# A delta-rule attention and router kernel: triangular inversions joined in pairs, in the room of the first expert's weights

## The chip, the cores and the metric

The kernel runs on one core of one Trainium2 chip. A core has a matrix engine (TensorE, PE), three engines for elementwise work (VectorE or DVE, ScalarE or ACT, GpSimd or POOL) and a queue that mostly issues DMA transfers (SyncE, SP). The metric is the device time of one execution in microseconds. Several executions are made, and their median is the time of a kernel. The profile is of one execution, and it has its own time and its own span.

## The reference

Everything is float32. First an attention block with a state: 4 batches, 8 heads, 768 tokens, head dimension 48. Each head carries a 48 by 48 state that is changed at every token:

```python
k_n = k / (np.linalg.norm(k, axis=-1, keepdims=True) + 1e-06)
for t in range(S):
    kt, vt, bt = (k_n[:, :, t], v[:, :, t], beta[:, :, t, None])
    y[:, :, t] = np.einsum('bhd,bhde->bhe', q[:, :, t], state)
    v_old = np.einsum('bhde,bhd->bhe', state, kt)
    state = state + bt[:, :, :, None] * np.einsum('bhd,bhe->bhde', kt, vt - v_old)
```

The result, put together over the heads, is `x` with 3072 rows of 384. Then comes a mixture of 8 experts. A router computes `x @ w_gate + log1p(exp(x @ w_noise)) * noise` for each row and takes the two largest; their weights are a softmax over the two. An expert computes `relu(x @ w1[e]) @ w2[e]` with 1024 hidden values, and each row's output is the weighted sum of its two experts.

## The kernel before

**Chunks, units, steps.** The attention is computed in chunks of 64 tokens. Inside a chunk the recurrence becomes a triangular system; between chunks only the state is carried. A unit is one chunk of two batches with all heads (128 rows), so each of the 12 chunks has 2 units. Two chunks are a step: 6 steps of 4 units.

**Work of a unit.** PE transposes k (L594, copied by ACT at L601) and multiplies k with itself (L612). The products' 32 by 32 blocks on the diagonal go to `gd` (L645), those beside it to `at`. After the inversion, `join` (L821, L827) puts two 32-blocks together to a 64-block; `within` transposes q and forms the masked products `qk` (L864). `recur` is the part that depends on the state: the old state's part of v (L612, then a subtraction on DVE, L914), the state's part of the answer (L885), the solve (L930, copied by ACT at L941), the gather of the new state (L952) and its addition on DVE (L964). v is multiplied by the norms of k on POOL (L894). `answer` computes the rows (L989), stores them to `rows_y`, turns them (L999) and multiplies them with the router's weights (L1004).

**The inversion.** One step's triangular blocks are inverted on DVE for all 32 units and heads at once. `gd` is transposed in 32 by 32 blocks into `t` (L662). A few small operations find the length of each k (L683 to L704), POOL clears one triangle (L712), a scale follows (L731), and then 30 columns of two instructions each: a product into `part` (L743) and an addition to `t` (L747). After the ends (L756, L759), two transposes write `tb` (L770) and `tt` (L778), which `join` reads. The list `INVERSIONS` says which steps are inverted together, as pairs of first step and number of steps; the tile `t` has a dimension for that number. Before, it is six times one step:

```python
INVERSIONS = [(s, 1) for s in range(6)]
```

**Routing and early tiles.** `route(g)` runs after some of the steps (`ROUTES`: after step 1, 3, 4 and 5, counted from 0). It picks the experts of the rows so far and scatters row numbers and weights into `tokens_x` with indirect DMAs on POOL (`spread`, L437, two per unit). The first five row tiles of expert 0, the early tiles, are computed in the same list of work: their metas are loaded, their rows gathered (L401), turned (L1294), multiplied (L1313), put through relu (L1324), multiplied back (L1337) and weighted (L1349). `put_early` adds a tile to the output.

**The order of work.** All of this is a list of jobs in the class `Jobs`. Each job has an engine, a cost, what it reads and writes, and perhaps a due time. `order` is a planner: it goes through a modelled time, and on each engine takes the job with the smallest key among those that can start. `FIRST`, `PACE` and `BEHIND` give the due times, `SLOW` multiplies PE's costs, and `PATIENCE`, `SOON`, `AFTER` and `APART` adjust the choice. The order that comes out is written to all five queues as it stands, so an instruction that waits holds back whatever is behind it on its engine. Buffers for kp, kT, v, q, norms and others are rings of fixed lengths. The weights of expert 0, `w1e` and `w2e` (1.5 MB each), are loaded during step 3. The output is cleared by four transfers (`clear_out`), and `blanks` fills `tokens_x`.

**After attention.** `rest()` is the seam: it loads the metas of all experts, gathers the remaining rows of expert 0 (`rest_x`) and the rows of expert 1 (`load_rows`), regroups them in sixteen transfers (L1562), forms sums of weight blocks on POOL, makes the puts that were held back, and multiplies the rest of expert 0 (L1686, L1697, L1707, L1712). Experts 1 to 7 follow with a scheme that needs fewer products (L1548).

Of the kernel before, what the change touches and what calls it, by code (L numbers as in the profile page):

```python
# [9 lines left out]
FP32 = mybir.dt.float32  # L10
# [11 lines left out]
Q = 32  # L22
# [5 lines left out]
EARLY_TILES = 5  # L28
PUT_IN_RULE = 1
# [6 lines left out]
FIRST, PACE, BEHIND = 15.0, 44.0, 110.0  # L36
INVERSIONS = [(s, 1) for s in range(6)]
# [59 lines left out]
class Jobs:  # L97
# [9 lines left out]
    SLOW = 1.3  # L107
# [5 lines left out]
    def add(self, engine, cost, emit, reads=(), writes=(), opens=None, uses=None, closes=None,  # L113
            lands=0.0, moves=0.0, due=None, late=None, apart=0.0):
# [3 lines left out]
            due=1e9 if due is None else due, late=late, apart=apart, after=set(),  # L118
# [24 lines left out]
    def order(self):  # L143
# [4 lines left out]
        for job in jobs:  # L148
            job.key = (0, job.due) if job.late is None else (1, job.late)
# [5 lines left out]
        ready = [0.0] * len(jobs)  # L155
# [66 lines left out]
    AFTER = 5.0  # L222
    APART = 2.0
    PATIENCE = 0.02
    SOON = 8.0
# [8 lines left out]
def kernel(  # L234
# [178 lines left out]
    early_x = [const.tile([128, DM], FP32, name=f"early_x{i}") for i in range(4)]  # L413
# [52 lines left out]
    def deltanet(ictx):  # L466
# [34 lines left out]
        NK, NT_, NW = 3 * US, 3 * US - 1, US + NU  # L501
# [21 lines left out]
        gd_all = sb([128, UH, Q], "gd")  # L523
        most_steps = max(x for _, x in INVERSIONS)
        inversion_of = {s + x: g for g, (s, n) in enumerate(INVERSIONS) for x in range(n)}
        t_invs = ring([128, most_steps, Q, Q], "t", 2)
        parts = sb([128, most_steps * 240], "part")
        tts, tbs = sb([128, UH, Q], "tt"), sb([128, UH, Q], "tb")
        norms = ring([128, UH], "norms", 3)
# [10 lines left out]
        def load_beta():  # L540
            by_block = beta.rearrange("(u b) h (s c n j) -> b n c u h s j", b=2, c=2, n=2, j=Q)
            for i in range(128 // H):
                b, n, c, u = i // 8, i // 4 % 2, i // 2 % 2, i % 2
                jobs.add(
                    SP, 0.7,
                    lambda i=i, at=(b, n, c, u): nc.sync.dma_start(  # L546
# [5 lines left out]
        def load(n, name):  # L552
            c, u = divmod(n, NU)
            src, t, size = {"k": (k, kps, NK), "q": (q, qps, NQ), "v": (v, vs, NQ)}[name]
            if name == "k":
                for i in range(2):
                    for z in range(2):
# [3 lines left out]
                            engine, 0.5,  # L561
# [25 lines left out]
        def turned(n, name, src, size, to, to_size):  # L587

            p = bank(1, True)

            def emit():
                p_t = p.tile.rearrange("p (j t) -> p j t", t=128)
                for j in range(NP):
# [6 lines left out]
                ACT, 0.6,  # L600
                lambda: nc.scalar.copy(  # L601
                    to(n), p.tile.rearrange("p (j t) -> p j t", t=128)
                ),
# [17 lines left out]
        def products(n):  # L621
# [6 lines left out]
            p = bank(2, True)  # L628
# [9 lines left out]
            for x, lo in enumerate(range(0, 128, Q)):  # L638
                rows, cols = slice(lo, lo + Q), slice(lo % C, lo % C + Q)
                on, copy = (DVE, nc.vector.tensor_copy) if s == 0 and x % 2 else (  # L640
                    ACT, nc.scalar.copy
                )
# [609 lines left out]

        def flat(p):
            return p.tile if p.size == 1 else p.tile[:, 0]

        def early(s, lo, hi):


# [622 lines left out]
```

## Time and profile before

| what | value |
|---|---|
| times of the runs shown | 811.42, 812.33, 818.18 us; median 812.33 |
| the profiled execution's own time | 819.58 us |
| its span | 817.8 us |
| mean granted PE clock | 0.897 |
| PE busy | 727.6 us |
| DVE busy | 566.7 us |
| ACT busy | 311.6 us |
| POOL busy | 414.3 us |
| first early product (L1313) on the chain | 319.07 us |
| first product of expert 1 on the chain (L1548) | 395.57 us |

The span runs from the first to the last instruction in the trace; the execution's own time is 1.8 us longer. The profiled execution took 7.3 us more than the median. Lines such as L743 are lines of the kernel before. A busy PE is not a PE at its peak: the granted clock says how fast it ran, and 0.50 means that a matmul takes about twice as long as at 1.00. The names before and after the arrow in a row are the tile that is written and the tiles that are read.

### The profile page before, as it was taken

How to read it: one execution, taken by the hardware profiler on the slowest of the kernel's cores; microseconds unless marked ns; L12 is line 12 of the kernel's file. 1: busy time of each engine (PE TensorE's matmuls, PEld its weight loads, DVE VectorE, ACT ScalarE, POOL GpSimd, SP SyncE). 2: the span in 40 equal slices, each digit the busy share in tenths (PEclk: the TensorE clock that was granted, in tenths of full speed). 3: DMA queues.
4: the chain of work that ended last, by engine and by line, in shares of the span. 5: the costliest groups of instructions: out<-in, count | busy, mean ns of one | idle time of the engine just before them, and what ended most of it. 6: DMA issues, size and time to landing. Idle time of an engine off the chain costs nothing.

```text
span 817.8 us, 22648 instructions
## 1 busy us (share of the span) xinstructions
PE 727.6 (89%) x9365; PEld 572.8 (70%) x9365; DVE 566.7 (69%) x1256; ACT 311.6 (38%) x740; POOL 414.3 (51%) x398
## 2 busy tenths in 40 slices
PE   4665887887889889999999999999999999999993
PEld 3445776676778779778568678578587597596693
DVE  4899889998899631303588487587686785785841
ACT  3547394846764542112250430430521511502500
POOL 2102100105520633569677786886886886787032
PEclk9955789768868656999999999999999999999998
DMA  2465636633333102464645444553445346333031
GB/s 47 78 111 126 184 96 157 175 73 67 61 72 71 43 23 40 156 105 84 183 112 120 126 132 83 146 154 56 144 142 104 100 138 129 89 59 43 0 38 26
DMA packets 142928, 79.61 MB, mean 97 GB/s; under 512 B 118624, under 2 KB 139232, under 8 KB 141792
## 3 DMA queue, kind: packets, MB, share of 16 engines
q1 hardware_dynamic: 128096, 57.94, 27.1%
q0 software_dynamic: 12544, 19.75, 13.7%
q8 instruction: 75, 1.23, 0.7%
q10 hardware_dynamic: 2176, 0.39, 0.3%
q14 instruction: 37, 0.30, 0.2%
HBM read 49.85 MB, written 20.03 MB: 85 GB/s over the span
## 4 chain that ended last, share of the span: by engine, by line
PE 60%; DVE 21%; issue 10%; POOL 3%; SPq 2%; ACT 1%; DMA 0%; DVEq 0%; POOLq 0%; ACTq 0%
PE inner L1548 25%; PE outer L1548 14%; DVE part L743 6%; DVE t L747 5%; PE pair L1313 3%; PE pair L1337 3%; PE pair L612 2%; POOL out_dram L456 2%; PE inner L1659 2%; PE single L1004 1%; SPq L546 1%; DVE t L662 1%; DVE qk L864 1%; PE pair L989 1%; SPq L562 1%
## 5 line engine op out<-in xcount | busy, mean ns | idle before, releaser
L1615 ACT ACTIVATE hT<-inner 128x416 f32<-128x416 f32 x112 | 57.9, 517 | 260.8 <-PE inner L1548 259.4
L1609 DVE TENSOR_TENSOR hT<-hT,inner 128x416 f32<-128x416 f32 x182 | 105.6, 587 | 64.0 <-PE inner L1548 55.9
L456 POOL DMA_INDIRECT out_dram<-sums,metas_x x51 | 83.6, 1639 | 94.4 <-DVE sums L1448 67.1
L437 POOL DMA_INDIRECT tokens_x<-meta,slot x48 | 48.7, 1014 | 97.8 <-DVE t L756 33.0
L1548 PE MATMUL inner<-s_x,w1e 128*128 128x416 f32 x196 | 78.7, 512 | 0.0
L743 DVE TENSOR_TENSOR part<-t 128x30 f32<-128x30 f32 (+9 forms) x180 | 69.2, 384 | 4.7
L747 DVE TENSOR_TENSOR t<-t,part 128x30 f32<-128x30 f32 (+9 forms) x180 | 64.3, 357 | 6.2
L1604 ACT ACTIVATE hT<-hT 128x416 f32<-128x416 f32 x112 | 59.9, 547 | 12.1 <-DVE hT L1609 6.8
L401 POOL DMA_INDIRECT xr<-rows_y,metas_x x49 | 56.4, 1152 | 14.0 <-issue 13.0
L712 POOL TENSOR_SCALAR_AFFINE_SELECT t<-t 128x1024 f32<-128x1024 f32 x6 | 7.6, 1268 | 107.5 <-DVE ss L683 107.5
L1548 PEld LDWEIGHTS inner<-s_x,w1e 128*128 128x128 f32 x196 | 37.2, 190 | 31.2 <-issue 29.0
L1548 PE MATMUL inner<-xe,w1e 128*128 128x416 f32 x140 | 58.1, 513 | 0.0
L1548 PE MATMUL outer<-t_w,hT 128*128 128x192 f32 x336 | 58.0, 326 | 0.0
L1548 PE MATMUL inner<-s_x,s_w 128*128 128x416 f32 x140 | 56.9, 512 | 0.0
L1548 PEld LDWEIGHTS outer<-t_w,hT 128*128 128x128 f32 x336 | 55.2, 190 | 0.0
L1514 POOL TENSOR_TENSOR w1e<-w1e 128x256 f32<-128x256 f32 x63 | 53.5, 858 | 2.3
L1548 PE MATMUL outer<-w2e,hT 128*128 128x192 f32 x280 | 50.7, 328 | 0.3
L1548 PEld LDWEIGHTS outer<-w2e,hT 128*128 128x128 f32 x280 | 46.1, 190 | 4.3 <-issue 2.2
L894 POOL TENSOR_TENSOR v<-v,norms 128x384 f32<-128x384 f32 x24 | 22.8, 967 | 46.3 <-DVE norms L726 25.5
L1548 PEld LDWEIGHTS inner<-s_x,s_w 128*128 128x128 f32 x140 | 26.6, 190 | 22.3 <-issue 22.3
L1548 PEld LDWEIGHTS inner<-xe,w1e 128*128 128x128 f32 x140 | 26.4, 190 | 20.7 <-issue 16.2
L801 ACT COPY w<-tt 32x256 f32<-32x256 f32 x96 | 38.6, 402 | 5.5 <-DVE tt L778 3.5
(191 smaller groups left out, 1594.1 us busy)
## 6 DMA issues: line engine op xcount, KB each, us to landing
w1e<-in_moe_w_dram SPq DMA_DIRECT2D x8, 1536.0 KB
w2e<-in_moe_w_dram SPq DMA_DIRECT2D x8, 1536.0 KB
xq<-xr SPq DMA_DIRECT2D x56, 84.0 KB
qp<-in_q_dram SPq DMA_DIRECT2D x48, 96.0 KB
v<-in_v_dram SPq DMA_DIRECT2D x48, 96.0 KB
out_dram<-empty SPq DMA_DIRECT2D x4, 1152.0 KB
rows_y<-y SPq DMA_DIRECT2D x24, 192.0 KB
kp<-in_k_dram SPq DMA_DIRECT2D x88, 48.0 KB
```

The source lines that it names most:

```text
L401: d = nc.gpsimd.indirect_dma_start(out=got, out_offset=None, in_=rows_y[0 : units * 128], in_offset=bass.IndirectOffsetOnAxis(ap=index, ax ...
L437: d = nc.gpsimd.indirect_dma_start(out=tokens_x, out_offset=bass.IndirectOffsetOnAxis(ap=slot, axis=0), in_=meta, in_offset=None, bounds_c ...
L456: d = nc.gpsimd.indirect_dma_start(out=out, out_offset=bass.IndirectOffsetOnAxis(ap=index, axis=0), in_=got, in_offset=None, bounds_check= ...
L743: v_.tensor_tensor(out=part, in0=t[:, :, j + 1 :, j, None].to_broadcast(shape), in1=t[:, :, None, j, 0:j].to_broadcast(shape), op=ALU.mult,)
L747: columns[:] = [v_.tensor_tensor(out=t[:, :, j + 1 :, 0:j], in0=t[:, :, j + 1 :, 0:j], in1=part, op=ALU.add).ins]
L801: lambda rows=rows, cols=cols, w64=w64, tt=tt: nc.scalar.copy(w64[rows, :, cols], tt[rows]),
L1313: nc.tensor.matmul(flat(p)[:, 0:rows], w1e[:, do, fo * 128 : (fo + 1) * 128], early_xe[:, do, 0:rows], start=(do == 0), stop=(do == KT - 1),)
L1514: engine.tensor_tensor(out=block(to), in0=block(x), in1=block(y), op=ALU.add if sign == "+" else ALU.subtract,)
L1548: nc.tensor.matmul(p, lhsT, rhs, start=opens and i == 0, stop=i == len(products) - 1, skip_group_check=True,)
L1604: nc.scalar.activation(h, h, ACTF.Relu)
L1609: nc.vector.tensor_tensor(out=h, in0=h, in1=p, op=ALU.add if sign > 0 else ALU.subtract)
L1615: nc.scalar.mul(h, p, float(sign))
```

## The change

- **Joined inversions.** `INVERSIONS` becomes `[(0, 1), (1, 2), (3, 2), (5, 1)]`: steps 1 and 2, and steps 3 and 4, counted from 0, are each inverted by one set of instructions of twice the width.
- **Room.** `t`, `part` and `gd` lie inside the weight tiles of expert 0. Its weights are loaded once the last inversions have been read: `w1e` after the transposes of step 4, `w2e` after those of step 5. The early tiles' hidden values share the room of `tt` and `tb`; `blanks` shares that of `early_xe`. `early_x` has five tiles instead of four; the rings of kp and kT grow to 16, that of norms to 6.
- **Start.** Half of the beta loads move from SP to POOL. For the first step, DVE copies kT, and the `gd` copies go by whole units, two to DVE and two to ACT.
- **Planner.** Its constants change, `begin` times come in, and the rule for a job's key. The early tiles' meta loads and row gathers become jobs of their own (`early_rows`) with due times.
- **Seam.** Metas of experts 1 and 0, then the rows of expert 1, then `rest_x`; the regroup's transfers alternate between SP and ACT; the other metas follow. All five puts come after the POOL sums (three before). `WITHIN` is empty, so what depends on it does nothing.

```diff
 EARLY_TILES = 5
-PUT_IN_RULE = 1
+WEIGHTS = 300.0
+WITHIN = {}
+EASY = 1, 0.7, 1, 0
+SOONER = -20, 0, -50, 10
+PUT_IN_RULE = -1
 ROWS = TILES * 128 + MORE
...
-FIRST, PACE, BEHIND = 15.0, 44.0, 110.0
-INVERSIONS = [(s, 1) for s in range(6)]
+FIRST, PACE, BEHIND = 13, 32, 145
+INVERSIONS = [(0, 1), (1, 2), (3, 2), (5, 1)]
...
     SIGNAL = 0.4
-    SLOW = 1.3
+    SLOW = 1.05
...
         for job in jobs:
-            job.key = (0, job.due) if job.late is None else (1, job.late)
+            job.key = (0, job.due) if job.due < 1e8 else (1, job.late or 0.0)
         waits = [len(job.after) for job in jobs]
...
                 then[i].append(job.number)
...
-    AFTER = 5.0
-    APART = 2.0
-    PATIENCE = 0.02
-    SOON = 8.0
+    AFTER = 0
+    APART = 1.3
+    PATIENCE = 0.01
+    SOON = 5.48
...
-        NK, NT_, NW = 3 * US, 3 * US - 1, US + NU
+        NK, NT_, NW = 4 * US, 4 * US, US + NU
...
         }
-        gd_all = sb([128, UH, Q], "gd")
         most_steps = max(x for _, x in INVERSIONS)
+        held = {"puts": [], "w": weight_tiles(w_even)}
+        room_1, room_2 = (
+            t.rearrange("p a b -> p (a b)") for t in held["w"]
+        )
+        of_t = most_steps * Q * Q
+        gd_all = room_1[:, of_t : of_t + UH * Q].rearrange("p (h q) -> p h q", q=Q)
         inversion_of = {s + x: g for g, (s, n) in enumerate(INVERSIONS) for x in range(n)}
-        t_invs = ring([128, most_steps, Q, Q], "t", 2)
-        parts = sb([128, most_steps * 240], "part")
-        tts, tbs = sb([128, UH, Q], "tt"), sb([128, UH, Q], "tb")
-        norms = ring([128, UH], "norms", 3)
+        t_two = [
+            x[:, 0:of_t].rearrange("p (s i j) -> p s i j", s=most_steps, j=Q)
+            for x in (room_1, room_2)
+        ]
+        parts = room_2[:, of_t : of_t + most_steps * 240]
+        def t_invs(g):
+            return t_two[g % 2]
+        of_joins = sb([128, 2, UH, Q], "tt_tb")
+        tts, tbs = of_joins[:, 0], of_joins[:, 1]
+        norms = ring([128, UH], "norms", NS)
         rows_of = [slice(i * C, (i + 1) * C) for i in range(2)]
...
                 b, n, c, u = i // 8, i // 4 % 2, i // 2 % 2, i % 2
+                engine, queue = ((SP, nc.sync), (POOL, nc.gpsimd))[i % 2]
                 jobs.add(
-                    SP, 0.7,
-                    lambda i=i, at=(b, n, c, u): nc.sync.dma_start(
+                    engine, 1.0 if i % 2 else 0.7,
+                    lambda i=i, at=(b, n, c, u), queue=queue: queue.dma_start(
                         out=beta_b[i * H : (i + 1) * H], in_=by_block[at]
...
-            p = bank(1, True)
+            first = name == "k" and n < US
+            p = bank(1, not first)
+            on, copy = (DVE, nc.vector.tensor_copy) if first else (ACT, nc.scalar.copy)
...
             jobs.add(
-                ACT, 0.6,
-                lambda: nc.scalar.copy(
-                    to(n), p.tile.rearrange("p (j t) -> p j t", t=128)
-                ),
+                on, 0.6,
+                lambda: copy(to(n), p.tile.rearrange("p (j t) -> p j t", t=128)),
                 writes=[(name + "T", n % to_size)], closes=p,
...
             turned(n, "k", kps, NK, kTs, NT_)
-            p = bank(2, True)
+            p = bank(2, s > 0)
             jobs.add(
...
             gd = gd_all.rearrange("p (u j z) i -> p u z j i", u=US, z=2)[:, i]
-            for x, lo in enumerate(range(0, 128, Q)):
+            on, copy = (DVE, nc.vector.tensor_copy) if s == 0 and i % 2 == 0 else (
+                ACT, nc.scalar.copy
+            )
+            for lo in range(0, 128, Q):
                 rows, cols = slice(lo, lo + Q), slice(lo % C, lo % C + Q)
-                on, copy = (DVE, nc.vector.tensor_copy) if s == 0 and x % 2 else (
-                    ACT, nc.scalar.copy
-                )
                 jobs.add(
-                    on, 0.38,
-                    lambda rows=rows, cols=cols, copy=copy: copy(
+                    on, 0.4,
+                    lambda rows=rows, cols=cols: copy(
                         gd[rows], two_banks(p, C)[rows, :, :, cols]
...
                     lambda x=x: v_.transpose(out=norms(first_s + x), in_=norm[:, x]),
-                    reads=[n_key], writes=[("norms", (first_s + x) % 3)],
+                    reads=[n_key], writes=[("norms", first_s + x)],
                 )
...
                 )],
-                reads=[("norms", s % 3)], writes=v_key,
+                reads=[("norms", s)], writes=v_key,
             )
...
-            easy = lambda x: x if paced else 0.0
+            easy = lambda x: x * EASY[g]
             jobs.add(
...
                 writes=["r_at", "r_d", "r_row", ("slot", g % 2)], closes=p,
-                due=FIRST + s * PACE + BEHIND,
+                due=FIRST + s * PACE + BEHIND - SOONER[g],
             )
...
                         ],
-                        reads=[("slot", g % 2), meta, ("num", g % 2), "blank"],
+                        reads=[("slot", g % 2), meta, ("num", g % 2), "blank", *looked_up],
                         writes=[("rows", of, i, y)], lands=2.0, moves=0.2,
...
         early_xe = sb([128, KT, 256], "early_xe")
-        early_hT = sb([128, FT, 256], "early_hT")
+        early_hT = of_joins.rearrange("p x h q -> p (x h q)").rearrange("p (f t) -> p f t", t=256)
...
-        def early(s, lo, hi):
...
-            w1e, w2e = held["w"]
+        def early_rows(s):
+            lo, upto = EARLY[s][0][0], EARLY[s][-1][1]
             of_steps = [
...
                 d = nc.sync.dma_start(
-                    out=early_meta[:, lo:hi],
-                    in_=tokens_x[lo * 128 : hi * 128].rearrange("(t p) c -> p t c", p=128),
+                    out=early_meta[:, lo:upto],
+                    in_=tokens_x[lo * 128 : upto * 128].rearrange("(t p) c -> p t c", p=128),
                 ).ins
...
             jobs.add(
-                SP, 0.7, load_meta, reads=of_steps, writes=[("early_meta", lo)], lands=2.0,
-                moves=0.3, late=lo,
-            )
+                SP, 0.7, load_meta, reads=of_steps, lands=2.0, moves=0.3, due=FIRST + s * PACE + BEHIND,
+                    writes=[("early_meta", i) for i in range(lo, upto)],
+                )
             units = (s + 1) * US
-            for i in range(n):
-                at = lo + i
-                x, x_key = early_x[at % 4], ("early_x", at % 4)
+            for at in range(lo, upto):
+                x, x_key = early_x[at], ("early_x", at)
                 jobs.add(
...
                     reads=[("early_meta", lo), *(("stored", i) for i in range(units))],
-                    writes=[x_key], lands=2.0, moves=0.7, late=lo,
-                )
+                    writes=[x_key], lands=2.0, moves=0.7, due=FIRST + s * PACE + BEHIND,
+                )
+        def early(s, lo, hi):
+            n, rows = hi - lo, (hi - lo) * 128
...
-        blanks = sb([128, E * N // 128, META], "blanks")
+        blanks = early_xe.rearrange("p k t -> p (k t)")[:, 0 : E * N // 128 * META].rearrange(
+            "p (t c) -> p t c", c=META
+        )
...
         behind(0, 20, 0.7, 1.0, lambda: blank(blanks), ["blank"])
-        held["w"] = weight_tiles(w_even)
         w1_even, w2_even = held["w"]
-        behind(3, 2, 0.7, 5.5, lambda: nc.sync.dma_start(out=w1_even, in_=w1r[0]), ["w1"])
-        behind(3, 15, 0.7, 5.5, lambda: nc.sync.dma_start(out=w2_even, in_=w2r[0]), ["w2"])
         for i in range(4):
...
             end_inversion(s)
+            if s + 1 == NS:
+                jobs.add(
+                    SP, 0.7, lambda: nc.sync.dma_start(out=w1_even, in_=w1r[0]), lands=2.0,
+                    writes=[
+                        "w1", ("t", 0),
+                        *(("gd", i, lo) for i in range(US) for lo in range(0, 128, Q)),
+                    ],
+                    moves=5.5, due=WEIGHTS,
+                )
+                jobs.add(
+                    SP, 0.7, lambda: nc.sync.dma_start(out=w2_even, in_=w2r[0]), lands=2.0,
+                    writes=["w2", ("t", 1)], moves=5.5, due=WEIGHTS + 20.0,
+                )
             for n in units:
...
                 cut(s, EARLY[s][-1][1] * 128)
+                early_rows(s)
         for s, batches in EARLY.items():
...
-        def regroup():
+        def regroup(queues=(nc.sync,)):
...
                 for c in range(QS):
-                    nc.sync.dma_start(
+                    queues[c % len(queues)].dma_start(
                         out=xq[c * Q : (c + 1) * Q, g, 0:tiles],
...
             got, gate = sums[0], metas_x[:, 0, :, 1]
-            for e in range(E):
-                load_metas(e)
+            load_metas(1)
+            load_metas(0)
+            load_rows(1)
             for i, size in enumerate(rows_in[t0:]):
                 take_rows(rest_x[0:size, i], place_of(metas_x[0:size, 0, t0 + i]), NT)
-            load_rows(1)
-            regroup()
+            regroup([nc.sync, nc.scalar])
+            for e in range(2, E):
+                load_metas(e)
             add_up(nc.gpsimd, SUMS_W, blocks[0])
```

## The prediction, made before the result was known

> **What bounds the kernel now.** I read the busy times first, then the chain, then stretches of it, then single instructions.
>
> ```profile
> PE 727.6 (89%) x9365; PEld 572.8 (70%) x9365; DVE 566.7 (69%) x1256; ACT 311.6 (38%) x740; POOL 414.3 (51%) x398
> ...
> PE 60%; DVE 21%; issue 10%; POOL 3%; SPq 2%; ACT 1%; DMA 0%; DVEq 0%; POOLq 0%; ACTq 0%
> ```
> The first line on the page lists engine shares one by one; the second is the chain by engine. PE carries 60% of what ended last, DVE 21%: two stages with different limits. The stretches (start:end, length, busy of PE, PEld, DVE, ACT, POOL, granted clock, DMA) show where they meet:
>
> ```profile
> 180.00:240.00 60.00, 51.22 (x1663) 45.00 (x1667) 52.65 (x120) 38.72 (x101) 27.89 (x29) 0.76 0.36 70
> 240.00:276.00 36.00, 28.44 (x911) 24.92 (x911) 33.68 (x100) 18.19 (x46) 4.11 (x4) 0.88 0.28 64
> 276.00:300.00 24.00, 20.16 (x639) 17.86 (x640) 7.88 (x29) 15.29 (x41) 16.35 (x19) 0.57 0.07 13
> 300.00:320.00 20.00, 19.92 (x394) 18.79 (x391) 4.95 (x19) 4.56 (x12) 2.10 (x3) 0.50 0.10 32
> ```
> To 276 DVE is 88 to 94% busy and PE has gaps; after 276 DVE rests and PE is the limit, at half clock. The chain names the turning point and the end of attention:
>
> ```profile
> 270.79 1.23 DVE t L759
> 272.05 1.93 DVE tb L770
> 274.06 1.07 PE single L821 x32
> ...
> 319.07 2.75 PE pair L1313 x6
> ...
> 395.57 4.74 PE inner L1548 x13
> ```
> The last inversion's transposes (L770, L778) release the last step's first join (L821) at 274.06. Attention ends at 319.07, where the early tiles of expert 0 begin. Expert 1 starts at 395.57, 76.5 us on; from there 422.2 us to the span's end (817.8), which the change doesn't touch. So the question is when attention's PE work ends.
>
> [...] clean columns of L743 and L747 take 0.19 us at 30 elements and 0.41 at 240, 1.048 ns an element and 0.16 fixed, and start 0.035 after the one before ends. Joining saves the fixed part only.
> [...] L894 began on POOL at 70.31:
>
> ```profile
> 69.73 0.38 DVE L747 TENSOR_TENSOR t<-t,part 128x210 f32<-128x210 f32 x1
> ...
> 70.56 0.90 DVE L747 TENSOR_TENSOR t<-t,part 128x220 f32<-128x220 f32 x1
> ```
> [...] from 300 to 320 PE is busy 19.92 of 20 us at 0.50. I keep both speeds for the tail.
> [...] The sixteen xq transfers took 10.47 us to issue on SP from 369.23.
>
> **The change, part by part.** (1) Two of six inversions fall into their neighbours.
>
> ```profile
> L743 DVE TENSOR_TENSOR part<-t 128x30 f32<-128x30 f32 (+9 forms) x180 | 69.2, 384 | 4.7
> L747 DVE TENSOR_TENSOR t<-t,part 128x30 f32<-128x30 f32 (+9 forms) x180 | 64.3, 357 | 6.2
> ```
> One inversion is 60 columns' operations, (69.2+64.3)/6 = 22.25 us. A joined pair does the same elements in 60 instructions instead of 120: 60×(0.16+0.035) = 11.7 us saved, 23.4 for two. The ten small operations on lengths (L683 to L704, 2.24 us) save about 1.7 a pair, 3.4; scale and ends (L731, L756, L759) about 0.5, 1.0. In all 27.8 us off DVE before the last inversion ends.
> (2) Against it, four kT copies go from ACT to DVE, 0.66 each (estimate from ACT's 0.587 and the gd copies, 0.423 on DVE against 0.365), 2.6 us; at the start DVE waited 8.2 us for ACT's gd copies, so they lie in that wait, or cost 2.6. Half of the beta loads leave SP: 8×(0.61 to 0.65+0.05) = 5.4 us sooner for what is queued behind. They now stand on POOL, ahead of nothing needed before 24. gd comes about 2.5 us sooner (18.9 to 16.3).
> (3) When steps become joinable (their L770/L778), by adding these prices along the new DVE order: step 0 at 55 (62 before), step 1 at 112 (98), step 2 at 131 (142), step 3 at 193 (188), step 4 at 212 (233), step 5 at 241 (274), ±4. The last: 274-27.8-2.5 for gd = 244, less some 3 for v and st updates (L914, L964, 0.55 each) that now stand behind it. Steps 1 and 3 come later, since a pair ends together; the rest sooner.
> (4) PE's work doesn't shrink; its order moves. At half-clock prices (a block of 16 matmuls of L612, L930, L952, L989 about 1.05 us, L885 0.95, six L1004 1.4, four L594 1.05) there are 43.6 us behind step 5's first join before the change, which took 45 (274.06 to 319.07): a ratio of 1.03. In the changed order seven units' recurrences stand behind it instead of four: 73.6. Behind step 1's join there were 249.8, done in 221: a ratio of 0.885, 15.6% of it gaps.
> I take 24 us of the 73.6 at 1.03, as much as ran near half clock before (296 to 320), and the other 49.6 at 0.8, between the busy ratio of the middle (0.747) and the whole (0.885): 24.7+39.7 = 64.4, end at 241+64 = 305. At 0.75 throughout: 296. At 1.03: 317. Cross-check from step 3's join, behind which 132 us stand at half-clock prices: 193 + 132×(0.8 to 0.9) = 299 to 312. Taken: 305, 14 us sooner.
> (5) Weights of expert 0 go into tiles that hold t, part and gd. Their loads (1.5 MB each) wait on SP for the last L778 of steps 4 and 5; v and q loads are queued behind. At about 212 and 241 they are free, and the early tiles need them at 305: over 40 us of cover. v behind the first lands about 8 us after it and is wanted about 10 after: nothing taken, 3 us at the most if late.
> (6) Spreads of route 1 (16×1.29 us = 21 us on POOL, L437) stand in one block ahead of v×norms (L894) of the last step; PE has 31 us of half-clock work there: free, or up to 6 us at full clock. The four clear-outs of the output (1.15 MB each, about 15 us together at 300 GB/s, a rate that this trace reaches around 100) come back to back ahead of q and v loads: 0 to 5. The early tiles' meta loads and row gathers get due times and so move up; the first meta load waits on SP for route 0's sixteen spreads, with k, q and v loads behind it: 0 to 3. I take nothing for all three, since PE has other units' blocks meanwhile, and keep their upper ends for the range.
> (7) The seam. PE keeps its sequence. Rows of expert 1 are gathered ahead of rest_x, about 4 us sooner, and the regroup's issue falls from 10.5 to 5.3. But PE is busy from 319 to 395.6 but for about 3 us, so 1 us either way. On ACT the eight issues stand behind the early relus and ahead of xe_r's copy (L1690), for which PE waits: up to 2 us lost. Metas of experts 2 to 7 move behind; they have 58 us each. Two more put_early calls (1.64 us each) move behind the POOL sums: 3.3 us, nobody waits. Taken: 0, range −1 to +2.
> (8) More rings for kp, kT, norms and early_x only take waits away; planner constants act through the order counted above.
>
> **The sum.** Profiled execution 819.58 (span 817.8, 1.8 around it): 817.8−14 = 803.8 of span, 805.6 with the surroundings. The shown runs' median is 812.33, 7.3 below that execution; the same 14 off it gives **798 us**.
>
> **The rivals.**
> - *Half clock to the end.* The unhidden tail of 73.6 us runs at 1.03 from 241: end 317, gain 2, **810 us**. For it: 300 to 320 at 0.50 though full. Against: the middle, with the same blocks, ran at 0.76 to 0.88.
> - *Full clock.* With DVE ahead, no waits and clock 0.9 or more: 73.6×0.64 = 47 from 241, end 288, gain 31; **781 us**. For: 240 to 276 had 0.88. Against: serial state, DVE's v and st between PE's blocks.
> - *Slower: the first pair starves PE.* Step 1 is joinable 14 us later, and all of PE's recurrence from there (228 us at half-clock prices, less than the 249.8 since more was done ahead) runs from 112. At the ratio of before, 0.885, it ends at 314 (within 1% of before). If the wait before it leaves PE at half clock and the clear-outs' burst holds the next loads, a ratio of 0.97 gives 333: 14 later, **826 us**. It decides above a ratio of 0.91, where the end passes 319.
> - *The joining doesn't show.* If POOL's blocking [...] doubles wide columns as it did narrow ones, the saving could be halved: step 5 joinable at 255, end near 319, 812. Against: L894 (24) and L712 (6) stay as many.
>
> **The numbers.** Forecast 0.52 (785 to 805), half clock 0.17, full clock 0.12, starved 0.13, no show 0.06. A measurement of this kernel tells about 1% from no change: 804.2 and 820.5 are the bounds. Faster: forecast bar 0.03, and the full clock, with little of the half clock: 0.64. Slower: most of the starved: 0.12. Within: 0.24. The range leaves out the fastest and the slowest tenth: 782 to 815.
>
> **What would show it.** L743 and L747 at 120 instructions each, together near 110 us instead of 133.5; last L778 between 237 and 248 instead of 274; the first L1313 near 305; the start of expert 1's L1548 minus that still 76 to 78; clock and gaps from 241 on, which decide between the cases. Wrong if PE waits at 100 to 125 for step 1 or for loads, if L1313 waits for w1, or if the seam grows.

## The result, and the profile after

The kernel after takes 807.15 us against 814.58 us (medians of twelve executions each, taken alongside). The ratio is 0.9896, with a 95% interval of 0.9859 to 0.9932: about 8.5 us faster, between 5.5 and 11.5. Two slow executions of the kernel after, 821.13 and 2337.13 us, count in its median but not in the ratio; with the first of them the gain would be about 7 us. The ratio is just beyond the 1% that the prediction took as the bound, though its interval reaches inside it, and the gain is three fifths of the 14 us that were forecast.

The two profiled executions differ by more: 817.8 us of span before, 803.1 after, 14.7 us. Busy times and the chain by engine, kernel after:

```profile
PE 711.0 (89%) x9365; PEld 557.9 (69%) x9365; DVE 542.0 (67%) x1114; ACT 308.2 (38%) x732; POOL 420.7 (52%) x410
...
PE 67%; DVE 13%; issue 11%; POOL 3%; ACT 2%; DMA 1%; ACTq 0%; SPq 0%; DVEq 0%; POOLq 0%
```

DVE's part of the chain fell from 21% to 13%, PE's rose from 60% to 67%. The inversions' column operations are L761 and L765 now (L743 and L747 before):

```profile
L765 DVE TENSOR_TENSOR w2e<-w2e 128x168 f32<-128x168 f32 (+28 forms) x60 | 26.7, 445 | 2.1
L761 DVE TENSOR_TENSOR w2e<-w1e 128x168 f32<-128x168 f32 (+28 forms) x60 | 26.6, 444 | 1.6
L761 DVE TENSOR_TENSOR w2e<-w2e 128x168 f32<-128x168 f32 (+28 forms) x60 | 26.5, 441 | 1.5
L765 DVE TENSOR_TENSOR w1e<-w1e,w2e 128x168 f32<-128x168 f32 (+28 forms) x60 | 26.1, 435 | 2.1
```

Together 105.9 us for 240 instructions, before 133.5 for 360. The stretches around the end of the inversions, kernel after (start:end, length, busy of PE, PEld, DVE, ACT, POOL, granted clock, DMA share, GB/s):

```profile
180.00:240.00 60.00, 46.90 (x1572) 40.29 (x1575) 44.84 (x104) 34.50 (x88) 26.67 (x26) 0.81 0.40 96
240.00:276.00 36.00, 31.71 (x1101) 28.72 (x1093) 16.77 (x47) 20.98 (x57) 6.64 (x7) 0.79 0.32 80
276.00:300.00 24.00, 19.68 (x659) 17.79 (x659) 10.63 (x37) 6.81 (x20) 14.82 (x17) 0.86 0.20 53
300.00:320.00 20.00, 19.46 (x236) 17.48 (x229) 7.07 (x40) 8.19 (x23) 8.98 (x9) 1.00 0.20 59
```

DVE falls from 94% to 47% busy in 240 to 276: the inversions are over there by now. PE still has idle time until 300, and the clock of each stretch from 240 on is 0.79 or more, where before it fell to 0.50. What half clock means can be read off the six early products that begin the next stage: 2.75 us before, at about 0.50, and 1.40 us after, at 1.00. The last step's first transpose on DVE, and the two marks on the chain, the first early product (L1348) and the start of expert 1 (L1596):

```profile
241.87 2.13 DVE L788 STREAM_TRANSPOSE tt_tb<-w2e 128x1024 f32<-128x1024 f32 x1
```
```profile
307.14 1.40 PE pair L1348 x6
...
380.33 28.13 PE inner L1596 x80
```

That transpose came 30 us sooner (272.05 before), the early products 12 (the first one starts at 307.0 after, at 318.9 before), expert 1 15. From there to the end it is 422.8 us, against 422.2.

### The profile page after: what moved, and what is told of

The parts are those of the page before. It is cut to its first block, busy times and chain, and to the rows that moved or that the text cites. A ratio compares the mean times of both kernels' runs of the same rounds, so it can differ in the third digit from the quotient of the medians.

```text
span 803.1 us, 22505 instructions
## 1 busy us (share of the span) xinstructions
PE 711.0 (89%) x9365; PEld 557.9 (69%) x9365; DVE 542.0 (67%) x1114; ACT 308.2 (38%) x732; POOL 420.7 (52%) x410
## 3 DMA queue, kind: packets, MB, share of 16 engines
q10 hardware_dynamic: 3968, 1.03, 0.6%
## 4 chain that ended last, share of the span: by engine, by line
PE 67%; DVE 13%; issue 11%; POOL 3%; ACT 2%; DMA 1%; ACTq 0%; SPq 0%; DVEq 0%; POOLq 0%
PE inner L1596 26%; PE outer L1596 14%; DVE w2e L761 4%; PE pair L1348 3%; PE pair L630 3%; PE pair L1372 3%; PE pair L1007 2%; POOL out_dram L460 2%; DVE w1e L765 2%; PE pair L970 2%; PE pair L948 2%; PE inner L1707 2%; PE single L1022 2%; PE single L614 2%; DVE w2e L765 2%
## 5 line engine op out<-in xcount | busy, mean ns | idle before, releaser
L1596 PE MATMUL inner<-s_x,w1e 128*128 128x416 f32 x196 | 78.7, 512 | 0.0
L441 POOL DMA_INDIRECT tokens_x<-meta,slot x48 | 50.6, 1055 | 39.9 <-DVE r_d L1095 16.7
L405 POOL DMA_INDIRECT xr<-rows_y,metas_x x49 | 56.3, 1149 | 20.4 <-issue 13.6
L1596 PEld LDWEIGHTS inner<-s_x,w1e 128*128 128x128 f32 x196 | 37.2, 190 | 31.2 <-issue 29.0
L1596 PE MATMUL inner<-xe,w1e 128*128 128x416 f32 x140 | 58.1, 513 | 0.0
L1596 PE MATMUL outer<-t_w,hT 128*128 128x192 f32 x336 | 58.0, 326 | 0.0
L1596 PE MATMUL inner<-s_x,s_w 128*128 128x416 f32 x140 | 56.9, 512 | 0.0
L1596 PEld LDWEIGHTS outer<-t_w,hT 128*128 128x128 f32 x336 | 55.2, 190 | 0.0
L1596 PE MATMUL outer<-w2e,hT 128*128 128x192 f32 x280 | 50.7, 328 | 0.3
L1596 PEld LDWEIGHTS outer<-w2e,hT 128*128 128x128 f32 x280 | 46.1, 190 | 4.3 <-issue 2.2
L1596 PEld LDWEIGHTS inner<-s_x,s_w 128*128 128x128 f32 x140 | 26.6, 190 | 22.3 <-issue 22.3
L1596 PEld LDWEIGHTS inner<-xe,w1e 128*128 128x128 f32 x140 | 26.4, 190 | 20.7 <-issue 16.4
L819 ACT COPY w<-tt_tb 32x256 f32<-32x256 f32 x96 | 38.6, 402 | 5.4 <-issue 2.3
L1596 PE MATMUL outer<-t_w,s_h 128*128 128x192 f32 x224 | 40.6, 329 | 0.0
L614 PE MATMUL single<-ident,kp 128*128 128x128 f32 x96 | 21.5, 365 | 21.2 <-ACT kT L621 9.8
L1492 DVE TENSOR_SCALAR sums<-outer,metas_x 128x192 f32<-128x192 f32 x70 | 27.8, 411 | 18.4 <-PE outer L1596 17.8
```

The lines of the kernel that those rows point to most:

```text
L405: d = nc.gpsimd.indirect_dma_start(out=got, out_offset=None, in_=rows_y[0 : units * 128], in_offset=bass.IndirectOffsetOnAxis(ap=index, ax ...
L441: d = nc.gpsimd.indirect_dma_start(out=tokens_x, out_offset=bass.IndirectOffsetOnAxis(ap=slot, axis=0), in_=meta, in_offset=None, bounds_c ...
L614: nc.tensor.transpose(p_t[:, j], src(n)[:, 2 * j : 2 * j + 2], ident)
L819: lambda rows=rows, cols=cols, w64=w64, tt=tt: nc.scalar.copy(w64[rows, :, cols], tt[rows]),
L1596: nc.tensor.matmul(p, lhsT, rhs, start=opens and i == 0, stop=i == len(products) - 1, skip_group_check=True,)
```

## The experiments

Ratios are to the kernel before, run beside each group of kernels on the same chip.

### Both kernels again: how much of the 14.7 us is the change

> The kernel before once more, for a second trace of it. The profiled execution of before was 5.0 us above its median of twelve, that of after 2.3 below its own, so the 14.7 us between the two spans would overstate the change. Theory A: the attention's PE stage is what varies from one execution to the next, with the granted clock; this trace then has its end of attention (first L1313) between 311 and 319, from the clock in 276 to 320, and the 422 us from expert 1 to the end unchanged within 0.5. Rival B: the expert stage varies; then the attention ends again at 319 and the 422 moves by some us.

> The kernel after once more. Theory A: from expert 1 on again 422 to 423 us; first L1348 between 304 and 316 against 307.0, later where the clock of the attention is lower; the last inversion's transposes (L788) again at 240 to 246, as DVE sets them. Rival B: the first L1348 again at 307 within 1 us, and the difference in the experts.

Nothing is edited. The kernel before has a span of 812.8 us this time, the kernel after 804.1. The last two stretches of the kernel before, second trace:

```profile
276.00:300.00 24.00, 20.83 (x718) 18.59 (x719) 9.06 (x28) 15.89 (x43) 15.66 (x19) 0.64 0.09 22
300.00:320.00 20.00, 19.92 (x312) 18.44 (x309) 5.08 (x21) 5.95 (x17) 5.49 (x6) 0.69 0.15 27
```

The clock was 0.57 and 0.50 in the first trace, and is 0.64 and 0.69 here, with PE as busy. The last inversion's transpose starts at 271.4 against 272.05, but the first early product at 313.5 against 318.9, and expert 1 to the end takes 422.4. For the kernel before theory A fits: the end of attention differs between the two executions, and so does the clock. For the kernel after it missed. The last inversion's transpose starts at 235.8, outside the expected 240 to 246, and the first early product at 307.2, as in the first trace; the expert stage, which rival B had in mind, is unchanged. After's clock in the last two stretches is 0.69 and 0.78 instead of 0.86 and 1.00, and the sooner inversion seems to have made up for it. The pair of second traces differs by 8.7 us, close to the timed 8.5. So 5.0 us of the 14.7 belong to the execution of before that the prediction was worked out on, and 1.0 to that of after.

### The kernel after without joining

```diff
-INVERSIONS = [(0, 1), (1, 2), (3, 2), (5, 1)]
+INVERSIONS = [(s, 1) for s in range(6)]
```

> The kernel after with six single inversions; room, rings, start, planner constants and seam as in after. Theory J, joining is the cause: DVE has some 27.6 us more before step 5's join, which comes at 262 to 275 instead of 244; time 0.995 to 1.015 of the kernel before. Rival R, the gain is from start, rings, order and seam: ratio 0.985 to 0.993, and step 5's join near 250.

Measured 1.0176 (1.0125 to 1.0228). Step 5's transpose starts at 268.1, 26 us later than after: joining gives DVE what was expected. The loss is a little larger than theory J's range, though its interval reaches into it, and rival R is excluded: the rest of the change, without joining, is worse than the kernel before. With that rest in place, joining is worth 2.8%. The early products start at 324.2, and from 276 to 300 PE is busy only 13.27 of 24 us.

### Joining alone, in the kernel before

```diff
-INVERSIONS = [(s, 1) for s in range(6)]
+INVERSIONS = [(0, 1), (1, 2), (3, 2), (5, 1)]
...
-        tts, tbs = sb([128, UH, Q], "tt"), sb([128, UH, Q], "tb")
+        of_joins = sb([128, 2, UH, Q], "tt_tb")
+        tts, tbs = of_joins[:, 0], of_joins[:, 1]
...
-        early_hT = sb([128, FT, 256], "early_hT")
+        early_hT = of_joins.rearrange("p x h q -> p (x h q)").rearrange("p (f t) -> p f t", t=256)
...
-                    writes=[("early_hT", fo)], closes=p, late=lo + 0.1,
+                    writes=[("early_hT", fo), "tt", "tb"], closes=p, late=lo + 0.1,
```

> The kernel before with the joined list of inversions alone (and the early tiles' hidden values in the room of tt and tb, so that the wider t and part find room); planner constants, rings, start, weights' loads and seam of before. Theory J, joining alone gives the gain where the order of work can follow: step 5's transposes about 25 us sooner, ratio 0.985 to 0.995. Rival P, joining without a remade plan leaves PE waiting for step 1 and 3 (both later by some 14 and 5 us), since PE's order was made with due times for single inversions: 0.998 to 1.015, with more PE gaps from 60 to 140 and after 276.

Measured 1.0567 (1.0497 to 1.0638), 46 us slower and far beyond both ranges; the direction is rival P's. Two stretches of this kernel:

```profile
60.00:100.00 40.00, 3.32 (x152) 2.66 (x149) 37.38 (x69) 6.41 (x17) 3.08 (x2) 0.50 0.46 146
100.00:140.00 40.00, 33.87 (x1309) 30.46 (x1309) 13.96 (x16) 31.22 (x78) 6.41 (x9) 0.74 0.42 92
```

PE is busy 3.3 of 40 us while DVE works through the first pair, and then DVE has little to do while PE catches up. The first of these stretches in the kernel before, and in the kernel after:

```profile
60.00:100.00 40.00, 26.31 (x928) 23.79 (x930) 36.47 (x79) 19.78 (x52) 6.28 (x6) 0.63 0.57 147
```
```profile
60.00:100.00 40.00, 28.96 (x1033) 24.99 (x1025) 36.96 (x67) 27.74 (x71) 3.23 (x4) 0.87 0.44 84
```

Three more lines of the kernel with joining alone say why: two of its waits (who waited for whom, us in total, times, longest), and one of DVE's timeline.

```profile
PE single L828 <- ACT w L802: 33.0, 1, 33.0
POOL v L895 <- DVE norms L727: 40.2, 1, 40.2
```
```profile
91.37 1.90 DVE L779 STREAM_TRANSPOSE tt_tb<-t 128x1024 f32<-128x1024 f32 x1
```

The `tt` transpose of step 0, 1.9 us of work, could have run at 56 and stands on DVE behind 25 of the pair's 30 columns. ACT's copies `w` need it, the join on PE (L828) needs them, and every recurrence of step 0 stands behind that. After, the same transpose runs at 52.1, ahead of the pair's columns. The transpose of step 0's norms (L727, at 96.69) stands behind all the columns, and POOL waits 40.2 us for it. So two small operations are caught here. Moving the first alone is not enough: in the two kernels of the next experiment it comes early, and PE starves as before. The second pair costs again: from 180 to 240 PE waits about 16 us for DVE's `qk`, `st` and `v`, against 2 in the kernel before.

### The kernel after with the old planner constants, and with three of them

```diff
-FIRST, PACE, BEHIND = 13, 32, 145
+FIRST, PACE, BEHIND = 15.0, 44.0, 110.0
```

This is the second kernel; the first also takes SLOW, AFTER, APART, PATIENCE, SOON, EASY and SOONER back to what gives before's behaviour.

> The kernel after with the planner's constants of before (SLOW, FIRST, PACE, BEHIND, AFTER, APART, PATIENCE, SOON and the two lists for routing); joined inversions, room, rings, start and seam of after. Theory P, half or more of the gain needs the remade order: ratio 0.996 to 1.01. Theory J, joining is what counts: 0.988 to 0.994.

> The kernel after with FIRST, PACE and BEHIND alone as before (15, 44, 110); all other constants as after. In DVE's order the four state updates of step 0 then come behind the whole first pair's columns, where after has them among its columns 14 to 22 of 30; from the third pair on the same again. Theory Q, these three due times alone decide whether the recurrence runs under a pair: PE nearly idle from 60 to 100, ratio 1.035 to 1.055, as with all constants of before (1.051). Rival, the loss there was SLOW's or SOON's: ratio 0.99 to 1.01.

Measured 1.0513 (1.0444 to 1.0583) and 1.0496 (1.0419 to 1.0572). The two ratios can't be set side by side as they stand: the second kernel's group ran under other conditions, with a slower kernel before and a cost that fell on these kernels (last section). What can be compared is the work up to 180 us, before the first spread. First the second kernel, then the first, then the kernel after:

```profile
0.00:180.00 180.00, 109.19 (x3137) 92.71 (x3138) 115.11 (x248) 99.32 (x256) 28.31 (x58) 0.67 0.43 95
```
```profile
0.00:180.00 180.00, 104.64 (x3148) 88.61 (x3148) 119.64 (x265) 100.27 (x258) 28.28 (x58) 0.73 0.44 98
```
```profile
0.00:180.00 180.00, 125.23 (x3713) 106.37 (x3713) 156.78 (x340) 113.45 (x294) 31.62 (x61) 0.79 0.47 104
```

With the three due times alone PE is as far behind, 3137 matmuls against 3713, as with all constants taken back (3148). So theory Q holds for the starving of PE; that the three also carry the whole 5% at the end is likely, but not shown. In the second kernel, on POOL (the bracket gives the idle time ahead of the instruction and what ended it):

```profile
93.74 5.28 POOL L912 TENSOR_TENSOR v<-v,norms 128x384 f32<-128x384 f32 x4 [39.14 <-DVE norms L744]
```

Here another small operation is caught behind the pair: the transpose of step 0's norms, 0.16 us, for which POOL's scaling of v waits 39 us, and PE's solve (L948) 29.1 us for that. PE is busy 5.4 of 40 us from 60 to 100. The kernel after with only these small operations moved, and all else kept, was not tried; that they are what starves PE is read from the waits.

### The seam of before in the kernel after

```diff
-PUT_IN_RULE = -1
+PUT_IN_RULE = 1
...
-            load_metas(1)
-            load_metas(0)
-            load_rows(1)
+            for e in range(E):
+                load_metas(e)
...
-            regroup([nc.sync, nc.scalar])
-            for e in range(2, E):
-                load_metas(e)
+            load_rows(1)
+            regroup()
```

> The kernel after with the seam of before: metas of all experts first, rest_x ahead of the rows of expert 1, the regroup on SP alone, and the puts of the first two early tiles before the POOL sums. Theory, seam worth 3 us (73.4 against 76.5 us from the first early product to expert 1 in the two traces): ratio 0.992 to 0.995, that stretch 76 to 77. Rival, as predicted, worth nothing: ratio 0.988 to 0.991, the stretch 73 to 74 because the early tiles, not the seam's order, gave the 3 us.

Measured 0.9891 (0.9848 to 0.9933), against 0.9896 for the kernel after: nothing that can be measured. From the first early product to expert 1 it takes 74.9 us; after took 73.3 and 74.1 in its two traces, before 76.6 and 76.9. The 1.7 us above after's first trace are not waits for the seam's transfers. They lie in one group of matmuls of the rest of expert 0, with the old seam and then in the kernel after:

```profile
L1745 PE MATMUL inner<-xe_r,w1e 128*128 128x192 f32 x42 | 8.9, 380 | 0.4 <-ACT xe_r L1738 0.4
```
```profile
L1747 PE MATMUL inner<-xe_r,w1e 128*128 128x192 f32 x42 | 7.3, 328 | 0.4 <-ACT xe_r L1740 0.4
```

The clock fell to 0.50 there for about 3 us. The second trace of before has the same dip (8.9), the first has not (7.3), with one and the same seam. So nothing is shown to come from the seam's order. The early tiles' own part can be read from what PE waited for ahead of the early products, before and then after:

```profile
PE pair L1313 <- ACT early_xe L1302: 1.2, 2, 0.6
```
```profile
PE pair L1348 <- ACT early_xe L1337: 0.2, 1, 0.2
```

PE waits 1.0 us less for turned rows, and three of the nine turning matmuls that stood in this stretch now come ahead of it: 1.5 us together. Three leftover transposes of attention (L999, 0.3 to 0.4) have moved out of it as well. These 1.9 us are in both pairs of traces. The rest is put down to the clock: in the first pair the six early products alone took 1.40 us at 1.00 instead of 2.75 at about 0.50. The change gathers those rows as jobs with due times, `early_rows`; that this is the reason was not tried alone.

### Less work on DVE without joining

```diff
             def column(j):
+                if j <= 5 or j >= Q - 6:
+                    return
```

> The kernel before, leaving out the ten short columns (the first five and the last five) of every inversion, so that the inverses are incomplete; order of work unchanged. About 5.6 us of DVE less an inversion, 34 in all, 28 of them before step 5's join. Theory D, DVE binds attention before the change: step 5's transposes at 245 to 255 instead of 271, the early products sooner by 10 to 20, ratio 0.976 to 0.988. Rival, PE and its order bind already: ratio 0.993 to 1.0.

> The kernel after with the same ten columns left out of every inversion: about 26 us of DVE less. Theory D, PE binds after the change and DVE no more: at most 6 us gained over after, ratio to the kernel before 0.981 to 0.990, PE's waits on DVE gone and PE busier. Rival, DVE still binds to step 5's join: another 12 to 20 us, ratio 0.965 to 0.975.

Before becomes 0.9759 (0.9678 to 0.984), after 0.9793 (0.9728 to 0.9858). For the kernel before theory D holds: about 28 us of DVE's work before step 5's join gave 20 us. Its transpose starts at 256.35, a little later than the 245 to 255 expected, and the early products at 297.2. The kernel after gains about 8.5 us over itself (0.9793/0.9896; with both intervals, taken as independent, between 2 and 15), more than theory D's 6 and less than the rival's 12: DVE still has a part there, and the ranges don't decide. Both end at the same place, 297.2 and 297.7, though DVE is freed at 256 and 231. From 240 to 276, before and after with less work:

```profile
240.00:276.00 36.00, 31.49 (x1086) 27.65 (x1085) 26.50 (x78) 20.20 (x54) 15.81 (x17) 0.89 0.25 53
```
```profile
240.00:276.00 36.00, 33.04 (x936) 29.86 (x929) 13.55 (x47) 18.19 (x49) 16.48 (x17) 0.69 0.33 86
```

DVE falls from 26.5 to 13.6 us and PE does no more for it; in the second, PE was busy longer at a lower clock. What less work on DVE buys in the kernel after is a lead: by 240 us PE has run 5683 matmuls, against 5282 and 5557 in the two traces of the kernel after.

### Pairs in other places, and less work early or late: what stays open

```diff
-INVERSIONS = [(0, 1), (1, 2), (3, 2), (5, 1)]
+INVERSIONS = [(0, 1), (1, 1), (2, 2), (4, 2)]
```

> The kernel after with the pairs put at steps 2 and 3 and at steps 4 and 5 instead of 1 and 2, 3 and 4: DVE's work is the same. Theory E, the early pair's lateness of step 1 (104 against 92 to 93) is what holds half of the saving back: step 1 ready near 85, step 5 near 230; ratio 0.978 to 0.987. Rival F, a step is always late by one single inversion somewhere, here 2 and 4, and the order was fitted to the other list: 0.99 to 1.01.

The last two kernels take the cut of ten columns for the first two inversions, or for the last two:

```diff
             def column(j):
+                if g <= 1 and (j <= 5 or j >= Q - 6):   # the other kernel: g >= 2
+                    return
```

> The kernel after with the ten short columns left out in the first two inversions alone (step 0, and the pair of steps 1 and 2): 12.9 us less of DVE before step 2, the later ones whole. Theory E, DVE holds PE back early, through the pair's lateness, and PE has the end of attention to itself: most of the 8 us that leaving out everywhere gave, ratio to the kernel before 0.978 to 0.985. Rival G, it is DVE's whole sum up to step 5 that counts: half of it, 0.983 to 0.988.

> The kernel after with the ten short columns left out in the last two inversions alone (the pair of steps 3 and 4, and step 5), again 12.9 us less. Theory E, as the prediction had it, PE binds behind step 5's join: at most 2 us, ratio 0.986 to 0.991, step 5's transposes 6 to 13 us sooner and the early products at most 2. Rival G: 4 us, ratio 0.983 to 0.987.

Measured 1.03 (1.0223 to 1.0377), 1.0117 (1.0068 to 1.0166) and 1.0248 (1.0208 to 1.0288): all three miss every range, the last two in spite of having less to do than the kernel after. The kernel before took 832.5 and 829.1 us beside them, 813.6 in the first two groups, so the conditions were others, and a further cost came in (last section). The kernel after itself was not run there. So these three times decide nothing between their theories: where the kernel after could still gain from DVE, early or late, is open. Two things can be read from the time before the first spread, where that cost does not come in. With the pairs in other places step 1's transposes came at 96.2, not near 85 as theory E had it. And by 175 us PE had run 3809 matmuls with less work early, the same lead as with less work everywhere (3784, against 3623 and 3660 in the two traces of the kernel after); what that lead is worth at the end is not shown. Within the last group, leaving out early was 13 us better than leaving out late, but that cost fell differently in the two.

## Why the prediction was right or wrong, point by point

**What bounds the kernel: right.** DVE held attention back until the last inversion: a DVE made shorter by leaving work out gave the kernel before 2.4%.

**Step 1, the price of joining: right in size, and partly by luck.** Forecast 110 us for the columns, measured 105.9; the saving on columns is 27.6 where 23.4 were forecast. Four kT copies took 0.69 us each (0.66 forecast). The 23.4 counted the gap of 0.035 us between two instructions, which is not busy time; the fixed part alone, 0.16, is 19.2 for 120 instructions. It is confirmed by undisturbed columns, one step before and a pair after, of 240 and 480 elements:

```profile
L743 DVE TENSOR_TENSOR part<-t 128x240 f32<-128x240 f32 x12 | 4.9, 408 | 0.4
```
```profile
L765 DVE TENSOR_TENSOR w2e<-w2e 128x480 f32<-128x480 f32 x2 | 1.3, 658 | 0.1
```

Twice 408 less 656 to 658 leaves 0.16 us. At this price all columns would take 119.1 us before and 99.9 after (an estimate from the undisturbed columns: 0.160 us and 1.033 ns an element). They took 14.4 and 6.0 more. That excess lies on the columns that ran beside an instruction of POOL, 51 of 360 before and 37 of 240 after; the others together are within 0.1 us of the price. So 8.4 of the 27.6 us are less delay beside POOL, which the prediction had named only as a danger; half of it is beside the clearing of the triangles (5.3 before, L712, and 1.0 after, L730).

**Step 3, when the steps become joinable: right.** Read as the prediction read the kernel before, by the end of the second transpose and for step 5 by that of the first, the times are 54, 108, 133, 191, 216 and 244; forecast 55, 112, 131, 193, 212, 241. The second trace has 54, 106, 133, 189, 214 and 238. But for step 1 in the second trace, all are within the ±4 that it gave, or at its edge. Step 1 is indeed later than before, and step 5 sooner by 30.

**Step 4, the tail on PE: right in length, not in make-up.** From 244 to 307 it took 63 us, 64.4 forecast; in the second trace, from 238 to 307, it took 69, so the close agreement is in part luck. The 24 us near half clock were not there; idle PE stood in their place (240 to 300: 51.4 of 60 us busy). Of the 9.1 us that PE idles from 240 to 307, under 1 us is a wait for another engine; in the rest it waits for nothing that the profile shows. So it is PE's own sequence that binds the tail, as the prediction had it, and in the second trace, at a lower clock, an inversion that ended 6 us sooner gained nothing. That the kernel after gained again with less work on DVE fits this: PE came to the tail with more done.

**The sum: the mis-sized term.** It reads "the same 14 off it": a saving from an end at 319.07 to one at 305, taken off the median of the runs. 319.07 was a late draw. That execution took 819.58, 5.0 above the median of twelve; the second trace ends attention at 313.5 with DVE's inversions at the same place. Against that, 307.2 is 6.3 us sooner, and with 2.8 from the seam and 0.4 given back in the experts that is the 8.7 us between the second traces. The term is mis-sized by 5.4 us, the difference between two executions of the same kernel, with the clock in the tail at 0.50 to 0.57 in the one and 0.64 to 0.69 in the other. The end at 305 itself was good: 307.0 and 307.2.

**Step 7, the seam: wrong by about 1 us beyond its bound.** Forecast 0, at best 1 shorter; it became 2.8 and 3.3 shorter in the two pairs of traces, of which about 1.9 is not the clock. The working looked at the seam's transfers. It left out the early tiles' turned rows, for which PE waited 1.2 us before, and that some of their matmuls could move ahead of this stretch. The transfers' order, which it priced at nothing, is not shown to give anything.

**Steps 5 and 6, the weights in the room of the inversions, and the queues: nothing shown against them.** In the trace of after no L1348 waits for w1. During the sixteen spreads of route 1 PE is busy 15.75 of 20.4 us there, about as much of the time as from 180 to 240 (46.9 of 60); the last section tells where it is not so.

**Step 8, rings and planner.** "Planner constants act through the order counted above" was right for the number. But the rival "starved" was described as something that clock and loads might bring about. It is decided by the order: joined without the new due times, PE is idle for 34 to 37 of 40 us (with joining alone at a granted clock of 0.50), and the kernel is 5% slower.

**The rivals.** Half clock to the end (810) and full clock (781) both spoke of the tail: after's clocks from 240 on, 0.69 to 1.00 in its two traces, lie between them. The joining that doesn't show is excluded by the columns.

## What to carry to other kernels

Making one instruction out of two saved one fixed cost here, 0.16 us, and the gap of 0.035 us behind it. But it made the first half's consumers wait for the second half (step 1 could be joined at 108 us instead of 98), and by the waits it was the small operations queued behind the wide ones that starved the other engines (POOL waited 40.2 us for one, PE 33.0 us for what stood behind another): look at what of the step before stands behind the pair, and have that come ahead. With the old order of work joining cost 5%; with the new one the whole change gave 1%. And before a saving is taken off a median, see where the profiled execution lies among the runs: two traces of the kernel before ended attention 5.4 us apart, and the whole effect is 8.5.

## What the runs showed of the hardware

In the last two groups (the kernel with three constants and those with pairs in other places, less work early and less work late) PE hardly issued while POOL issued its spreads (indirect DMAs, L441). The sixteen spreads of one route: first the kernel after in its own trace, then the kernel with less work late (same columns as above):

```profile
269.50:289.90 20.40, 15.75 (x628) 14.04 (x619) 5.04 (x16) 9.12 (x24) 15.81 (x17) 0.92 0.26 53
```
```profile
289.38:309.75 20.37, 6.73 (x84) 4.61 (x74) 0.61 (x4) 0.35 (x1) 15.80 (x16) 0.50 0.08 11
```

In the same 20.4 us PE ran 628 matmuls in one and 84 in the other, and POOL did the same work. The chain of the second inside it, and POOL's lines beside it:

```profile
298.08 0.46 PE pair L1009 x3
298.54 0.97 issue
299.51 0.47 PE pair L1009 x3
299.97 0.96 issue
300.93 0.35 PE pair L1009 x2
```
```profile
298.46 0.98 POOL L441 DMA_INDIRECT tokens_x<-meta,slot  x1 [0.30 <-issue]
299.75 0.98 POOL L441 DMA_INDIRECT tokens_x<-meta,slot  x1 [0.31 <-issue]
301.04 0.98 POOL L441 DMA_INDIRECT tokens_x<-meta,slot  x1 [0.30 <-issue]
```

PE runs a few matmuls and then pauses for about 1 us, waiting for nothing that the profile shows; the DMA engines are nearly idle (0.08), and one load of instructions falls into this block, where there are six in the first. The pauses don't keep step with single spreads: PE's bursts start 1.42 to 1.43 us apart here, the spreads 1.29. PE's busy time over the length of the block, for the unbroken blocks of sixteen spreads ahead of the early products, is 0.77 to 0.90 in the traces of the first two groups and of the timed pair, and 0.32 to 0.44 in the three kernels of the last experiment.

That it goes with the spreads is seen from all of them together. From 180 us to the first early product, PE began 5.5 to 8.5 matmuls a us inside the blocks of spreads and 23.7 to 27.8 outside them, in the four kernels of the last two groups. In the ten others it was 20 to 30 inside and 22 to 28 outside. In the expert stage nothing is seen of it: from expert 1 to the end the three kernels take 422.7 to 423.1 us as ever. What causes it was not found out. Each group ran on another chip, so whether it belongs to a chip or to its state at the time is open too. It was seen in blocks of spreads that stand in the middle of many short matmuls. The kernel before has such a block as well and took 15 to 19 us longer beside those kernels, though no trace of it was taken there; and the kernel's 1% was measured where it did not appear.
